# Solving the second group of four attention chunks in two half-size blocks, and filling in the corners by matmul

## The chip, the cores and the metric

One core of a Trainium2 chip runs the whole program. The metric is device time in microseconds (us). TensorE (PE) does the matmuls, VectorE (DVE), ScalarE (ACT) and GpSimd (POOL) the elementwise work, and SyncE (SP) issues most of the DMA transfers.

## The reference, cut to what matters

```
for t in range(768):                       # attention: B=4, H=8, D=40
    y[t]  = r[t] @ state
    Sa    = state @ a[t]
    state = state * w[t] - outer(Sa, b[t]) + outer(v[t], k[t])
x = y, as 3072 tokens of 320               # 8 heads x 40
x = ((x @ w1) * (x @ w2) @ w3) @ w_out     # 320 -> 1024 -> 1024 -> 320
h = max(x @ w_in, 0)                       # 320 -> 2048
out = (h * h) @ w_out2                     # 2048 -> 320
```

## The kernel before, in words

The attention runs in 24 chunks of 32 time steps. Inside a chunk the steps depend on each other through a triangular 32 by 32 system for each of the 32 pairs of batch and head. `solve(k, blocks)` inverts it ahead of time for four chunks at once, k=0 for chunks 0 to 3 and k=1 for chunks 4 to 7, and so on: four transposes in, a chain of steps on DVE (each a multiply, L666, and a subtract, L669), four transposes out. With blocks=1 the chain has 31 steps on the full triangle. With blocks=2 it has 15 steps, which treat the two 16 by 16 diagonal blocks side by side; two more transposes (`tnat`, L678) keep a copy in the other orientation, and `corner(c, i)` then fills the off-diagonal block of chunk c with two rounds of 64 small matmuls: L700 (i=0), whose result ACT scales into `x1` (L707), and L703 (i=1), whose result ACT copies into the solved tile (L711). Before the change k=0 uses two blocks, and the later solves one.

A chunk passes the stages x0, sa, sat, l, z, ys: `do_x0` (L752, ACT evicts X at L754), `do_sa` (L762, ACT copies SA at L764), `do_sat` (L769; ACT copies YI, L774, and vs, L771), `do_l` (L786, DVE writes YI, L791), `do_z` (L799, ACT copies YR, L802), `do_ys` (L814). At the end of ys DVE writes the new state, RX (L822), from which the next chunk's x0 starts, and the output yst (L826). So the chunks form one serial chain through PE, ACT and DVE. Chunks are prepared some way ahead: `prep` (scans on DVE, L564 and L574, products on POOL, L586 and L592), `prep_pq` (pq: PE L605, ACT L609, DVE L612) and `prep_kb` (kb: PE L624, ACT L628).

Between the stages the kernel works on the first feed-forward network. Early on that is `fold`, the product of w3 and w_out (PE L466, ACT L468, DVE L469), and the splitting of w1 and w2 into high and low parts: `fetch` (a DMA, L322, into `raw` or `early`; ACT L329 and L330; DVE L332 and L334), then ACT L344 for the high part and POOL L345 for the low one (`split_w`), and L357 and L358 for the last 64 rows (`split_r`). From chunk 3 on it is the matmuls `ab` (L374) and `px` (L432). After about 710 us the second network follows, on PE alone (`ph`, L374, and `po`, L1014).

The order of instructions on PE is that of the code; the table `BETWEEN` says which side works (prep, pq, kb, solve, corner) stand after which stage of chunks 0 to 3, and `pull` takes so many ns of feed-forward work. The orders on ACT, DVE, POOL and SP come from a scheduler with priorities, so a change in the table moves instructions there too, and each of these engines works its list in order.

Of the kernel before, what the change touches and what calls it, by code (L numbers as in the profile page):

```python
# [7 lines left out]
F32 = mybir.dt.float32  # L8
# [7 lines left out]
B, H, S, D = 4, 8, 768, 40  # L16
# [17 lines left out]
    (0, "start"): (("prep", 5), ("prep", 6)),  # L34
    (0, "x0"): (("corner", 0),),
    (0, "sat"): (("w3",), ("corner", 1, 0)),
    (0, "l"): (("pq", 5), ("corner", 1, 1)),
    (0, "ys"): (("kb", 5), ("pq", 6), ("kb", 6)),
    (1, "start"): (("prep", 7),),
    (1, "sat"): (("corner", 2, 0),),  # L40
    (1, "l"): (("corner", 2, 1),),
    (1, "ys"): (("pq", 7), ("kb", 7), ("solve", 1)),
    (2, "start"): (("prep", 8),),
    (2, "sat"): (("corner", 3, 0),),
    (2, "l"): (("corner", 3, 1),),
    (2, "z"): (("pq", 8), ("pull", 1300), ("kb", 8), ("pull", 1000)),
    (3, "start"): (("prep", 9),),
    (3, "z"): (("pq", 9), ("pull", 1300), ("kb", 9), ("pull", 1000)),
}
FOLD_NS = 535  # L50
SPLIT_AT = (8, 13)
# [193 lines left out]
def body(tc, img, rv, rd, vn, vp, raw, w1, w2, w3t, wo, win, wo2, ident, maskt, out, dbg=None):  # L245
# [4 lines left out]
    with (  # L250
# [12 lines left out]
        with right, tc.manual_schedule(engines={mybir.EngineType.PE}):  # L263
# [185 lines left out]
            def fold(solved):  # L449

                wf = tc.alloc_tile_pool(name="wf", bufs=1, side="right")
                wo_sb = wf.tile([128, 8, DM], F32, name="wo_sb", bufs=1)
                w3 = {}

                def load_w3(i):
                    f, g = i // 2, i % 2
                    w3[i] = fetch(wf, 4, 128, [(slice(0, 128), slice(0, 4), wcols(w3t, 128 * f, 128)[
                        512 * g:512 * g + 512, :].rearrange("(k p) f -> p k f", p=128))])

                def step(f, k):  # L460
                    if k == 0:
                        t = ps_ab.tile([128, 2, 256], F32, name="pw", tag="ab")
                        w3["ps"] = t.rearrange("p a t -> p (a t)")[:, 0:DM]
                    ps = w3["ps"]
                    i = 2 * f + k // 4
                    mm(out=ps, lhsT=w3[i][:, k % 4], rhs=wo_sb[:, k], start=(k == 0), stop=(k == 7))  # L466
                    if k == 7:
                        act.copy(out=wf_["h"][:, f], in_=ps)  # L468
                        dve.tensor_tensor(out=wf_["l"][:, f], in0=ps, in1=wf_["h"][:, f], op=ALU.subtract)  # L469

                def split12(j):
                    if not w12:
                        w12.extend([tuple(wa.tile([128, 2, FA], F32R, name=f"w{i}{n}") for n in "hl") + (
                            wa.tile([128, FA], F32R, name=f"w{i}r"),) for i in "12"])
                    for k in range(2):
                        for src, t in zip((w1, w2), w12):
                            split_w(wf, src, *t[0:2], j, k)
                    split_r(wf, [(src, 512 * j, t[2]) for src, t in zip((w1, w2), w12)])

                hold.append(solved)  # L480
                for i in range(8):
                    fetch(wf, 1, DM, [(slice(0, 128), 0, wcols(wo)[128 * i:128 * i + 128, :])], dst=wo_sb[:, i:i + 1])
                for i in range(3):
                    load_w3(i)
                hold.clear()
                items = []
                for f in range(8):
                    for k in range(8):
                        items.append((FOLD_NS, lambda f=f, k=k: step(f, k), "w"))
                        i = 2 * f + k // 4  # L490
                        if k % 4 == 3:
                            if i + W3_FIRST < 16:
                                items.append((0, lambda i=i + W3_FIRST: load_w3(i), "decode"))
                            for j in range(2):
                                if SPLIT_AT[j] == i:
                                    items.append((0, lambda j=j: split12(j), "decode"))
                return items + [(0, wf.release, "decode")], lambda: [load_w3(i) for i in range(3, W3_FIRST)]

            with (
# [134 lines left out]
                def solve(k, blocks):  # L634
# [39 lines left out]

                    def tnat(j):
                        if j == 0:
                            TT["nat"] = nat
                        dve.transpose(out=TT["nat"].rearrange("p u s -> p s u")[:, 8 * j:8 * j + 8],  # L678
                                      in_=square(T).rearrange("p t s -> p s t")[:, 8 * j:8 * j + 8])

                    items.append(init)
# [6 lines left out]

                def corner(c, i):

                    tn = TT["nat"][:, 8 * (c % 4):8 * (c % 4) + 8]
                    if i == 0:
                        TT["x1"] = ma.tile([128, H, 16], F32, name="x1", tag="x2")
                    x1 = TT["x1"]
                    ps = psat()
                    for h in range(H):
                        for b in range(B):
                            r = slice(32 * b, 32 * b + 32)
                            if i == 0:
                                mm(out=ps[r, 0, 16 * h:16 * h + 16], lhsT=Pn0[r, c % 4, h], rhs=TT[c][r, h, 16:32],  # L700
                                   start=True, stop=True, tile_position=(32 * b, 32 * b))
                            else:
                                mm(out=ps[32 * b:32 * b + 16, 0, 16 * h:16 * h + 16], lhsT=tn[r, h], rhs=x1[r, h],  # L703
                                   start=True, stop=True, tile_position=(32 * b, 32 * b))
                    v = ps[:, 0, 0:128].rearrange("p (h t) -> p h t", t=16)
                    if i == 0:
                        act.activation(out=x1, in_=v, func=AF.Copy, scale=-1.0)  # L707
                    else:
                        for b in range(B):
                            r = slice(32 * b, 32 * b + 16)  # L710
                            act.copy(out=TT[c][r, :, 16:32], in_=v[r])  # L711
# [149 lines left out]
                def run(what):  # L861
                    for op, *a in what:
                        if op == "prep":
                            prep(a[0], dve if a[0] in PD else pool)
                        elif op == "pq":
                            stage(prep_pq, a[0], a[0] % 4)
                        elif op == "kb":
                            stage(prep_kb, *a)
                        elif op == "corner":
                            for b in range(2):  # L870
                                if len(a) == 1 or a[1] == b:
                                    stage(corner, a[0], b)
# [281 lines left out]
```

## Time and profile before

| | |
|---|---|
| runs | 1073.35, 1070.08, 1073.58 us, median 1073.35 |
| profiled execution | 1070.06 us |
| its span, first to last instruction | 1068.2 us |
| around the span | 1.9 us |
| mean granted TensorE clock | 0.963 |
| PE, DVE, ACT, POOL busy | 917.6, 710.4, 441.9, 230.9 us |

The busy times are sums over the whole span, whose stages have different limits. The times in the rows count from the span's start, so an instruction at 118.97 us began 118.97 us after the first instruction.

### The profile page before, as it was taken

How to read it: one execution, taken by the hardware profiler on the slowest of the kernel's cores; microseconds unless marked ns; L12 is line 12 of the kernel's file. 1: busy time of each engine (PE TensorE's matmuls, PEld its weight loads, DVE VectorE, ACT ScalarE, POOL GpSimd, SP SyncE). 2: the span in 40 equal slices, each digit the busy share in tenths (PEclk: the TensorE clock that was granted, in tenths of full speed). 3: DMA queues.
4: the chain of work that ended last, by engine and by line, in shares of the span. 5: the costliest groups of instructions: out<-in, count | busy, mean ns of one | idle time of the engine just before them, and what ended most of it. 6: DMA issues, size and time to landing. Idle time of an engine off the chain costs nothing.

```text
span 1068.2 us, 29228 instructions
## 1 busy us (share of the span) xinstructions
PE 917.6 (86%) x12240; PEld 821.4 (77%) x12240; DVE 710.4 (67%) x1399; ACT 441.9 (41%) x943; POOL 230.9 (22%) x303
## 2 busy tenths in 40 slices
PE   1347686799989889879899999889999999999996
PEld 1235454688879779768898889878988988988886
DVE  8854889868966996896489345896455554444432
ACT  2533455343443334433343334785433333333332
POOL 0361124533334443323200000652000000000000
PEclk9999888899999999999899999989999999999999
DMA  8877775676667667656645443665123121000001
GB/s 240 297 227 200 215 225 148 157 190 163 149 151 185 161 153 192 166 155 153 161 119 111 127 97 67 174 193 99 30 62 68 46 46 25 2 25 1 24 3 27
DMA packets 209389, 134.44 MB, mean 126 GB/s; under 512 B 143793, under 2 KB 184114, under 8 KB 209252
## 3 DMA queue, kind: packets, MB, share of 16 engines
q1 hardware_dynamic: 201892, 110.61, 40.6%
q0 software_dynamic: 7072, 21.57, 7.1%
q8 instruction: 98, 1.61, 0.7%
q10 hardware_dynamic: 288, 0.33, 0.1%
q14 instruction: 39, 0.32, 0.1%
HBM read 99.27 MB, written 33.19 MB: 124 GB/s over the span
## 4 chain that ended last, share of the span: by engine, by line
PE 49%; DVE 24%; DMA 8%; issue 4%; ACT 4%; SPq 2%; POOL 2%; ACTq 0%; DVEq 0%; POOLq 0%
PE ph L374 16%; PE po L1014 15%; PE ab L374 6%; DVE T L669 4%; DVE tmp L666 3%; PE px L432 3%; DVE RX L822 2%; PE pat L814 2%; DVE yst L826 2%; DVE wst L332 2%; DMA X_d<-yst 2%; DVE wst L334 2%; DVE g L406 1%; DMA im<-img 1%; PE pat L786 1%
## 5 line engine op out<-in xcount | busy, mean ns | idle before, releaser
L1014 PE MATMUL po<-wul,rh 128*128 128x320 f32 x384 | 118.3, 308 | 0.0
L1014 PE MATMUL po<-wuh,rh 128*128 128x320 f32 x384 | 118.0, 308 | 0.0
L1014 PE MATMUL po<-wuh,rl 128*128 128x320 f32 x384 | 116.9, 308 | 0.7 <-DVE rl L1001 0.7
L411 ACT CAST gh<-g 128x256 fp32r<-128x256 f32 x96 | 38.8, 405 | 104.9 <-DVE g L406 92.5
L374 PE MATMUL ph<-xh,wih 128*128 128x512 f32 x192 | 76.0, 396 | 0.7 <-POOL wul L960 0.7
L374 PE MATMUL ph<-xh,wil 128*128 128x512 f32 x192 | 75.7, 394 | 0.0
L814 PE MATMUL pat<-YI,YR 128*40 128x72 f32 (+1 forms) x1536 | 59.0, 240 | 19.3 <-DVE qt L612 17.5
L374 PE MATMUL ph<-xl,wih 128*128 128x512 f32 x192 | 75.6, 394 | 0.0
L1014 PEld LDWEIGHTS po<-wul,rh 128*128 128x128 f32 x384 | 72.0, 188 | 4.2
L1014 PEld LDWEIGHTS po<-wuh,rh 128*128 128x128 f32 x384 | 72.0, 188 | 3.8
L814 PEld LDWEIGHTS pat<-YI,YR 128*40 128x40 f32 x1536 | 54.4, 127 | 24.9 <-DVE qt L612 19.5
L1014 PEld LDWEIGHTS po<-wuh,rl 128*128 128x128 f32 x384 | 71.6, 188 | 1.0 <-DVE rl L1001 0.9
L432 PE MATMUL px<-wph,gh 128*128 128x320 f32 x192 | 65.9, 343 | 6.9 <-ACT gh L411 3.8
L405 ACT COPY a_sb<-ab 128x256 f32<-128x256 f32 x96 | 35.6, 371 | 83.9 <-PE ab L374 83.3
L592 POOL TENSOR_TENSOR im<-im,suf 104x256 f32<-104x256 f32 x80 | 68.1, 879 | 4.7 <-DMA im<-img 2.5
L669 DVE TENSOR_TENSOR T<-T,tmp 128x31 f32<-128x31 f32 (+20 forms) x170 | 65.8, 387 | 3.1
L412 DVE TENSOR_TENSOR gl<-g,gh 128x256 fp32r<-128x256 f32 x96 | 46.9, 489 | 28.6 <-ACT gh L411 28.3
L666 DVE TENSOR_TENSOR tmp<-PT,T 128x31 f32<-128x31 f32 (+20 forms) x170 | 63.3, 372 | 3.4
L432 PE MATMUL px<-wph,gl 128*128 128x320 f32 x192 | 61.2, 319 | 2.3 <-DVE gl L412 2.2
L374 PE MATMUL ab<-xh,w1h 128*128 128x256 f32 x192 | 58.1, 303 | 2.9 <-ACT xh L361 1.9
L432 PE MATMUL px<-wpl,gh 128*128 128x320 f32 x192 | 60.5, 315 | 0.0
L374 PE MATMUL ph<-xq,wir 128*128 128x512 f32 x192 | 60.1, 394 | 0.0
(539 smaller groups left out, 2439.3 us busy)
## 6 DMA issues: line engine op xcount, KB each, us to landing
raw<-w3t SPq DMA_DIRECT2D x16, 512.0 KB
YR<-KB_d SPq DMA_DIRECT2D x48, 160.0 KB
im<-img POOLq DMA_DIRECT2D x28, 240.0 KB, 4.7
wt<-AW_d SPq DMA_DIRECT2D x24, 214.5 KB
raw<-wo SPq DMA_DIRECT2D x16, 320.0 KB
RX<-vp SPq DMA_DIRECT2D x24, 208.0 KB
vs<-rv SPq DMA_DIRECT2D x24, 208.0 KB
KB_d<-kn POOLq DMA_DIRECT2D x14, 320.0 KB, 5.1
```

Of the source, the lines that this page charges most:

```text
L332: dve.scalar_tensor_tensor(out=ou, in0=ou, scalar=3, in1=lo, op0=ALU.logical_shift_left, op1=ALU.bitwise_or)
L334: dve.scalar_tensor_tensor(out=ou, in0=hi, scalar=0x80000000, in1=ou, op0=ALU.bitwise_and, op1=ALU.bitwise_or)
L374: mm(out=ps, lhsT=seq[i][0], rhs=seq[i][1], start=(i == 0), stop=(i == 7))
L405: act.copy(out=a_sb, in_=ps[:, 0])
L411: act.copy(out=t["gh"][:, ff], in_=g)
L412: dve.tensor_tensor(out=t["gl"][:, ff], in0=g, in1=t["gh"][:, ff], op=ALU.subtract)
L432: mm(out=ps, lhsT=a_, rhs=b_, start=(k == 0 and i == 0), stop=(k == 7 and i == 2))
L592: eng.tensor_tensor(out=kb[:, g, :, :, j], in0=kb[:, g, :, :, j], in1=sg, op=ALU.mult)
L666: dve.tensor_tensor(out=tv, in0=Pv[:, :, s, s + 1:n].unsqueeze(3).to_broadcast(sh), in1=Tv[:, :, s, 0:s + 1].unsqueeze(2).to_broadcast(sh) ...
L669: return dve.tensor_tensor(out=o, in0=o, in1=tv, op=ALU.subtract).ins
L814: mm(out=ps[64 * y:64 * y + D, b, 72 * z:72 * z + n], lhsT=YR[:, u], rhs=YI[:, u, 0:n], start=True, stop=True, tile_position=(0, 64 * y))
L1014: mm(out=po[j][g], lhsT=a_, rhs=b_, start=(ff == 0 and i == 0), stop=(ff == 15 and i == 2))
```

## The change

The solve of chunks 4 to 7 goes in two blocks of 16, as that of chunks 0 to 3 did. Its corners are new: that of chunk 4 after stage ys of chunk 2, those of chunks 5, 6 and 7 between the stages of chunk 3. The corners of chunks 2 and 3, which stood between the stages of chunks 1 and 2, stand with chunk 0. The pq and kb of chunk 8 move from behind stage z of chunk 2 to behind its ys. In the split of w1 and w2 both halves of w1 come ahead of those of w2; they alternated. Two tiles change their places (`nat` of the second solve takes the buffer `x2`, `x1` one of the two of `a_sb`). The later solves are issued elsewhere in the code, in one block, before and after.

```diff
-    (0, "l"): (("pq", 5), ("corner", 1, 1)),
-    (0, "ys"): (("kb", 5), ("pq", 6), ("kb", 6)),
+    (0, "l"): (("pq", 5), ("corner", 1, 1), ("corner", 2, 0)),
+    (0, "ys"): (("corner", 2, 1), ("corner", 3, 0), ("kb", 5), ("corner", 3, 1), ("pq", 6), ("kb", 6)),
     (1, "start"): (("prep", 7),),
-    (1, "sat"): (("corner", 2, 0),),
-    (1, "l"): (("corner", 2, 1),),
     (1, "ys"): (("pq", 7), ("kb", 7), ("solve", 1)),
     (2, "start"): (("prep", 8),),
-    (2, "sat"): (("corner", 3, 0),),
-    (2, "l"): (("corner", 3, 1),),
-    (2, "z"): (("pq", 8), ("pull", 1300), ("kb", 8), ("pull", 1000)),
+    (2, "z"): (("pull", 2300),),
+    (2, "ys"): (("corner", 4, 0), ("pq", 8), ("corner", 4, 1), ("kb", 8)),
     (3, "start"): (("prep", 9),),
+    (3, "x0"): (("corner", 5, 0),),
+    (3, "sa"): (("corner", 5, 1),),
+    (3, "sat"): (("corner", 6, 0),),
+    (3, "l"): (("corner", 6, 1),),
     (3, "z"): (("pq", 9), ("pull", 1300), ("kb", 9), ("pull", 1000)),
+    (3, "ys"): (("corner", 7),),
...
-                    for k in range(2):
-                        for src, t in zip((w1, w2), w12):
+                    for src, t in zip((w1, w2), w12):
+                        for k in range(2):
                             split_w(wf, src, *t[0:2], j, k)
...
-                            TT["nat"] = nat
+                            TT["nat", k] = nat if k == 0 else ma.tile([128, 32, 16], F32, name="nat", tag="x2")
...
-                        TT["x1"] = ma.tile([128, H, 16], F32, name="x1", tag="x2")
+                        TT["x1"] = ma.tile([128, H, 16], F32, name="x1", tag="a_sb", bufs=2)
...
-                            marks[a[0]] = solve_all(a[0], 1 if a[0] else 2)
+                            marks[a[0]] = solve_all(a[0], 2)
```

Lines of the changed kernel are two higher than those named above. What the change moves is shown at three places. First PE, from the second corner round of chunk 1 (`x1_803`) to the first x0 matmuls of chunk 1 (into which `RX_97` goes). Before:

```order
L605 MATMUL pat_861<-im_601 32x64 x32
L703 MATMUL pat_899<-x1_803,early_103 16x16 x32
L814 MATMUL pat_937<-YI_509,YR_96 40x72 x16
L814 MATMUL pat_958<-YI_509,YR_96 40x72 x16
L466 MATMUL pw_981<-wo_sb_521,wst_565 128x320 x2
L624 MATMUL pat_990<-idt_63,im_601 128x104 x8
L605 MATMUL pat_1003<-im_105 32x64 x32
L624 MATMUL pat_1041<-idt_63,im_105 128x104 x8
```

After:

```order
L705 MATMUL pat_899<-x1_803,early_103 16x16 x32
L702 MATMUL pat_937<-tt_342,early_103 32x16 x32
L816 MATMUL pat_972<-YI_509,YR_96 40x72 x16
L816 MATMUL pat_993<-YI_509,YR_96 40x72 x16
L468 MATMUL pw_1016<-wo_sb_521,wst_565 128x320 x2
L705 MATMUL pat_1025<-x1_936,early_103 16x16 x32
L702 MATMUL pat_1063<-tt_342,early_103 32x16 x32
L626 MATMUL pat_1097<-idt_63,im_601 128x104 x8
L705 MATMUL pat_1110<-x1_1062,early_103 16x16 x32
L607 MATMUL pat_1147<-im_105 32x64 x32
L626 MATMUL pat_1185<-idt_63,im_105 128x104 x8
L754 MATMUL pat_1215<-RX_97,XL_511 32x40 x32
```

Four corner rounds, those of chunks 2 and 3, have come between the l stage of chunk 0 and x0 of chunk 1.

Second ACT at the start of chunk 1, whose x0 result is `X0_101`, whose SA is `SA_102`; `early` tiles hold loads of w1 and w2 (1737 and 1745 of w1, 1754 of w2), `kn` belongs to kb. Before:

```order
L628 COPY kn_991<-pat_990 128x8x40 x2
L609 COPY Pn_104<-pat_1003 128x2x4x32
L628 COPY kn_1042<-pat_1041 128x8x40 x2
L754 ACTIVATE X0_101<-pat_1071 128x320
L329 ACTIVATE wst_796<-raw_797 128x512
L329 ACTIVATE wst_1746<-early_1745 128x512
L330 ACTIVATE early_1745<-early_1745 128x512
L764 COPY SA_102<-pat_1112 128x8x40
L774 COPY YI_509<-SA_102 32x8x40 x4
```

After:

```order
L331 ACTIVATE wst_1738<-early_1737 128x512
L332 ACTIVATE early_1737<-early_1737 128x512
L630 COPY kn_1186<-pat_1185 128x8x40 x2
L331 ACTIVATE wst_1746<-early_1737 128x512
L332 ACTIVATE early_1737<-early_1737 128x512
L346 CAST w1h_1731<-wst_1738 128x512
L756 ACTIVATE X0_101<-pat_1215 128x320
L346 CAST w1h_1731<-wst_1746 128x512
L331 ACTIVATE wst_1755<-early_1754 128x512
L331 ACTIVATE wst_796<-raw_797 128x512
L346 CAST w2h_1734<-wst_1755 128x512
L766 COPY SA_102<-pat_1256 128x8x40
```

Both halves of w1's load and the cast of the first now stand ahead of X0, and the cast of a half of w2 ahead of SA.

Third ACT at the start of chunk 3 (X0 is again `X0_101`). `raw_2229` holds the last rows of the second column half of w1 and w2. Before:

```order
L344 CAST w1h_1739<-wst_2095 128x512
L468 CAST wph_70<-pw_1864 128x320
L329 ACTIVATE wst_1920<-raw_1921 128x512
L330 ACTIVATE raw_2121<-raw_2121 128x512
L754 ACTIVATE X0_101<-pat_2004 128x320
```

After:

```order
L709 ACTIVATE x1_1891<-pat_1892 128x128
L346 CAST w2h_1734<-wst_2219 128x512
L611 COPY Pn_104<-pat_1926 128x2x4x32
L331 ACTIVATE wst_2228<-raw_2229 128x512
L332 ACTIVATE raw_2229<-raw_2229 128x512
L713 COPY tt_1494<-pat_1964 16x8x16 x4
L630 COPY kn_2002<-pat_2001 128x8x40 x2
L359 CAST w1r_1733<-wst_2228 64x512
L359 CAST w2r_1736<-wst_2228 64x512
L756 ACTIVATE X0_101<-pat_2031 128x320
```

The decoding of raw_2229, the two casts of its rows (w1r, w2r), the four corner copies of chunk 4 and kb 8's copies now stand ahead of X0. On SP the load of raw_2229 stands behind the two writes of chunk 2's yst.

## Rows read from the trace of the kernel before

**Rows 1.** Windows by chunk: start, end, length, busy PE PEld DVE ACT POOL, clock, DMA.

```profile
93.30:124.60 31.30, 21.64 (x477) 15.44 (x476) 19.09 (x31) 18.42 (x38) 7.46 (x8) 0.89 0.78 218
124.60:174.50 49.90, 32.76 (x512) 23.16 (x512) 43.46 (x81) 24.45 (x48) 18.06 (x17) 0.88 0.73 212
174.50:203.40 28.90, 24.56 (x380) 19.31 (x380) 28.14 (x56) 12.84 (x26) 11.22 (x11) 0.86 0.49 133
203.40:710.00 506.60, 456.57 (x7960) 422.41 (x7960) 374.47 (x834) 215.07 (x518) 154.20 (x225) 0.95 0.60 150
```

**Rows 2.** Chain of waits, chunk 1 to chunk 3: start, us, what.

```profile
128.30 7.13 DMA xf<-X_d
...
159.94 0.49 DVE wpl L469
...
204.85 0.67 DVE tt L672
```

**Rows 3.** DVE timeline, chunk 2: start, us, line, tiles, idle before.

```profile
155.16 1.50 DVE L669 TENSOR_TENSOR T<-T,tmp 128x252 f32<-128x252 f32 x1
...
169.99 0.98 DVE L822 TENSOR_TENSOR RX<-pat,gc 40x320 f32<-40x320 f32 x2
```

**Rows 4.** Windows of L666: first solve, second solve, chunk 2 after xl.

```profile
29.00:50.50 21.50, 4.20 (x15) 1.00 0.87 284
125.00:206.00 81.00, 12.94 (x31) 0.87 0.65 185
136.10:169.90 33.80, 5.34 (x11) 0.90 0.69 211
```

**Rows 5.** The same windows, of L669.

```profile
29.00:50.50 21.50, 4.60 (x15) 1.00 0.87 284
125.00:206.00 81.00, 14.28 (x31) 0.87 0.65 185
136.10:169.90 33.80, 6.92 (x11) 0.90 0.69 211
```

**Rows 6.** Windows of all engines, chunk 2 after xl.

```profile
136.10:169.90 33.80, 24.31 (x363) 17.29 (x362) 31.45 (x52) 21.68 (x43) 12.73 (x12) 0.90 0.69 211
```

**Rows 7.** PE timeline, kb 5, a corner round, ys of chunk 3.

```profile
90.72 0.88 PE L624 MATMUL pat<-idt,im 104*128 104x104 f32 x8
...
109.46 0.69 PE L703 MATMUL pat<-x,early 32*16 32x16 f32 x64 [2.90 <-ACT x L707]
...
197.12 3.41 PE L814 MATMUL pat<-YI,YR 128*40 128x72 f32 x64 [2.96 <-DVE qt L612]
```

**Rows 8.** SP timeline, the load of half of w1.

```profile
93.48 0.41 SPq L322 DMA_DIRECT2D early<-w  x1
```

**Rows 9.** ACT timeline, chunk 1 and x0 of chunk 2.

```profile
94.24 0.44 ACT L754 ACTIVATE X<-pat 128x320 f32<-128x320 f32 x1
...
99.66 0.66 ACT L329 ACTIVATE wst<-early 128x512 f32<-128x512 f32 x1 [3.52 <-DMA early<-w]
...
100.77 0.41 ACT L764 COPY SA<-pat 128x320 f32<-128x320 f32 x1
...
103.09 0.58 ACT L771 COPY vs<-pat 104x512 f32<-104x512 f32 x1
...
111.68 1.04 ACT L711 COPY tt<-pat 16x128 f32<-16x128 f32 x4
...
130.81 0.67 ACT L330 ACTIVATE raw<-raw 128x512 uint32<-128x512 uint32 x1 [4.98 <-DMA raw<-w3t]
```

**Rows 10.** DVE timeline, chunk 1.

```profile
111.17 1.39 DVE L791 TENSOR_TENSOR YI<-pat,msk 64x512 f32<-64x512 f32 x2
...
118.97 0.99 DVE L822 TENSOR_TENSOR RX<-pat,gc 40x320 f32<-40x320 f32 x2 [2.03 <-PE pat L814]
```

**Rows 11.** ACT timeline, X0 of chunk 3.

```profile
176.26 0.44 ACT L754 ACTIVATE X<-pat 128x320 f32<-128x320 f32 x1 [6.49 <-PE pat L752]
```

**Rows 12.** POOL timeline, the first halves of w2l.

```profile
153.39 2.99 POOL L345 TENSOR_TENSOR w2l<-wst,w2h 128x512 fp32r<-128x512 f32 x2 [14.66 <-PE pat L703]
```

More of the change, by code (lines that the diff above doesn't have):

```diff
@@ L676, in tnat @@
                         if j == 0:
-                            TT["nat"] = nat
-                        dve.transpose(out=TT["nat"].rearrange("p u s -> p s u")[:, 8 * j:8 * j + 8],
+                            TT["nat", k] = nat if k == 0 else ma.tile([128, 32, 16], F32, name="nat", tag="x2")
+                        dve.transpose(out=TT["nat", k].rearrange("p u s -> p s u")[:, 8 * j:8 * j + 8],
                                       in_=square(T).rearrange("p t s -> p s t")[:, 8 * j:8 * j + 8])
@@ L689, in corner @@
                 def corner(c, i):
-                    tn = TT["nat"][:, 8 * (c % 4):8 * (c % 4) + 8]
+                    tn = TT["nat", c // 4][:, 8 * (c % 4):8 * (c % 4) + 8]
                     if i == 0:
-                        TT["x1"] = ma.tile([128, H, 16], F32, name="x1", tag="x2")
+                        TT["x1"] = ma.tile([128, H, 16], F32, name="x1", tag="a_sb", bufs=2)
                     x1 = TT["x1"]
@@ L699, in corner @@
                             if i == 0:
-                                mm(out=ps[r, 0, 16 * h:16 * h + 16], lhsT=Pn0[r, c % 4, h], rhs=TT[c][r, h, 16:32],
+                                mm(out=ps[r, 0, 16 * h:16 * h + 16], lhsT=(Pn if c > 3 else Pn0)[r, c % 4, h], rhs=TT[c][r, h, 16:32],
                                    start=True, stop=True, tile_position=(32 * b, 32 * b))
```

## The prediction, made before the changed kernel ran

> **What bounds the kernel now.** I read the windows by chunk first, then the chain of waits, then the timelines of the engines that it names. From 203 us on the kernel is PE's: 456.57 of 506.60 us busy [rows 1], and the work of that part is not changed, so what counts is when chunk 4 gets there. Ahead of it PE is busy for two thirds of the time (21.64 of 31.30 us in chunk 1, 32.76 of 49.90 in chunk 2), while DVE is busy for 43.46 of the 49.90 us of chunk 2 and for 28.14 of the 28.90 us of chunk 3 [rows 1]. The chain of waits says the same: after the load of xf ahead of chunk 2's feed-forward work, at 128.30 us, it passes through PE, and from 159.94 us to the last transpose out of the second solve at 204.85 us every named piece is DVE's [rows 2]. So DVE bounds chunks 2 and 3, and handovers through ACT and DMA bound chunk 1. I follow five points: X0 of chunk 1 at 94.24 us [rows 9], the first RX of chunk 1 at 118.97 us [rows 10], that of chunk 2 at 169.99 us [rows 3], X0 of chunk 3 at 176.26 us [rows 11], and the end of chunk 3's ys at 197.12 + 3.41 = 200.53 us [rows 7].
>
> **What DVE saves.** The second solve takes 12.94 + 14.28 = 27.22 us in its 62 steps, the first, in two blocks, 4.20 + 4.60 = 8.80 us in 30 [rows 4, 5]. That is 18.4 us less. Two further transposes of about 0.6 us each (an estimate, from the 0.67 us of a transpose out [rows 2]) leave 17.2. The question is how much of it the chain of chunks can use.
>
> **Chunk 0.** Four corner rounds now stand between l of chunk 0 and x0 of chunk 1. A round takes 0.69 us on PE [rows 7], so four take 2.8. They alternate with ACT's evictions, and I add one wait of about 0.9 us where the second round of chunk 3 comes close behind its eviction; the one such wait shown is 2.90 us [rows 7], but kb 5 stands between here. Term: +3.7, bounds +2.8 and +5.7. In chunks 1 and 2 the rounds that go away lay in PE's idle time, so I credit nothing there, and 2.8 as the bound.
>
> **Chunk 1.** X0 stood on ACT behind kb's copies. Now it stands behind the decoding of both halves of w1 and one cast. Their load waits on SP for the tile that kb 5's transposes and the corners read, and those end 3.7 later than 90.72 + 0.88 [rows 7], at 95.3. The load of a half was issued at 93.48 us [rows 8] and used at 99.66 [rows 9]: 6.2 us. So the halves land at about 101.5 to 102, and four ACT instructions of 0.66, two copies and a cast later X0 starts at about 105 in place of 94.24, +10.8. SA follows behind two casts and a decode at 107.4 to 110, in place of 100.77 [rows 9], and vs, behind buffers that POOL must free, at 112 to 116 in place of 103.09 [rows 9]. From there part is absorbed: before, l's result lay ready at about 105.3 and DVE wrote it to YI only at 111.17 [rows 10], so 5.9 us of the delay fit into a wait that was there. YR then stands behind further loads of w1 and w2. The first RX comes between 122.2 and 127.8, against 118.97 [rows 10]; I take the middle, 125.0, that is +6.0, because the load waits of this chunk (3.52 us for one [rows 9]) are neither the shortest nor the longest that it can meet. Beyond chunk 0's 3.7 this adds **+2.3**, bounds -0.5 and +5.1.
>
> **Chunk 2.** From the first RX of chunk 1 the chain goes through yst, X_d and xf (128.30 + 7.13 = 135.43 [rows 2]) to xl on DVE at about 136.1. This is not changed. From 136.1 to 169.9, 33.8 us, DVE is busy for 31.45 [rows 6]; 22 steps of the solve are 5.34 + 6.92 = 12.26 of it [rows 4, 5]. Afterwards 21 of the 30 shorter steps stand there, at 8.80 / 30 = 0.29 us each, 6.15. Now the whole solve stands ahead of RX, with four transposes more (+2.5), two decode instructions and one qt fewer (-1.8). Sum: 31.45 - 12.26 + 6.15 + 0.7 = 26.0 us busy. The 2.35 us that DVE waited I leave, which gives 28.3 in place of 33.8: **-5.5**, bound -7.8 if those waits go too. Some steps here are stretched: one of 252 columns took 1.50 us [rows 3] while POOL was in w2l from 153.39 for 2.99 us [rows 12], and 22 steps took 0.56 us on average, against 0.44 over all 62 (27.22 / 62) [rows 4, 5]. If the short steps meet the same POOL work the stretch of 22 x 0.12 = 2.6 us stays, -2.9: the upper bound.
>
> The Trainium skill, page "SBUF — State Buffer", section "SBUF: two separate sides", says that a DVE instruction with two SBUF inputs and a GpSimd instruction that reads SBUF hold one port pair exclusively, each for its whole length. The 1.50 us step beside w2l agrees. By that rule the wait doesn't shrink with the step, and the sum below would be 2.6 us higher.
>
> **X0 of chunk 3.** Before it came 176.26 - 169.99 = 6.3 us after the first RX of chunk 2 [rows 3, 11]. Now it stands on ACT behind the last rows of w1 and w2, whose load on SP follows the two writes of yst. RX and yst of both halves take about 3.7 us (the same four groups follow each other from 118.97 [rows 10] to 122.7). Three issues of 0.41 [rows 8] are 1.2. The load is half as large as the one that took 6.2, I take 5.0 (3.1 if it went by bytes). ACT then decodes it in two instructions, 1.3, copies tt for chunk 4, 1.04 [rows 9], and kn and two casts, four instructions of 0.4 to 0.66, 2.0. Sum 14.2, so **+7.9**, bounds +6.0 and +9.1.
>
> **Chunk 3.** Before, from X0 to the end of ys it took 200.53 - 176.26 = 24.3 us, DVE being full. Afterwards DVE has no solve here, and PE's work of this stretch is what bounds it: about 17.2 us with corners 5 and 6 (4 rounds, 2.8) and without those fold matmuls that now run ahead of X0, plus some 3 us of handovers. 20.3 in place of 24.3: **-4.0**, bounds -6 and 0. Corner 7 then stands ahead of x0 of chunk 4; its first round is partly hidden behind RX: +0.4. Corner 7 also ends the list: with PE busy for nine tenths from there on, the shift stays as it is.
>
> **The sum.** 3.7 + 2.3 - 5.5 + 7.9 - 4.0 + 0.4 = +4.8 us. On the profiled execution's own 1070.06 us this gives 1074.9. The median of the runs, 1073.35, lies 3.3 above that execution, so I predict 1078.2. A difference under 0.3%, 3.2 us, is about what a measurement of this kernel can't tell from none.
>
> The term of chunk 3's X0 and that of chunk 1 rest on ACT working its list in order. A row shows it: ACT waited 4.98 us for a load of w3t at 130.81 [rows 9], with X0 of chunk 2 in the list behind it. The Trainium skill, page "TensorE: Matmul & The Clock Gate", table of specifications, calls the queues of ScalarE, VectorE and GpSimdE strict FIFO, which agrees. If work could pass a waiting load, those two terms would vanish and the sum would be -5.4.
>
> **Rivals.** *Faster: the relief of DVE comes through.* If w1 lands in time, so that X0 of chunk 1 is no later than chunk 0's 3.7 (97.9 us), and if the last rows of w1 and w2 land within 6.3 us of RX, the chunks get the 17.2 us, less 3.7 for chunk 0, less 3.2 for corners 5 to 7: -10.3, 1063. For it speaks that DVE is the only engine in the chain for 45 us [rows 2]. Against it, both loads stand behind work that ends too late. Chance 0.28.
>
> *No change.* Chunk 1 absorbs all but the lower bound (-0.5) and chunk 2 gains its full 7.8: 3.7 - 0.5 - 7.8 + 7.9 - 4.0 + 0.4 = -0.3, 1073. For it speaks the 5.9 us wait of YI, which may cover more than I allow. Chance 0.18.
>
> *Slower by more.* The loads in chunk 1 queue behind each other and POOL's stretch stays: +5.1 and -2.9 in place of +2.3 and -5.5, +10.2, 1083.5. Speaks for it the DMA share of 0.78 in chunk 1 [rows 1], which is the highest of these windows. Chance 0.10.
>
> My own case has 0.44, with a range of 1074 to 1083. Of it I count 0.06 to no change, at its lower edge. So: faster 0.28, same 0.24, slower 0.48. The range that leaves out 2 in 10 runs from 1062 to 1085.
>
> **What would show it.** The two-block solve: 15 instructions each of multiply and subtract, 8 to 10 us in all. Chunk 1: X0 near 105, SA after 107, RX near 125. Chunk 2: RX 45.5 us after chunk 1's. X0 of chunk 3 about 14 us after that, with a wait for the DMA of raw ahead of it on ACT; ys ends 20 us later. The wait of w2l on corner 3 (14.66 us [rows 12]) is gone. I am wrong if X0 of chunk 1 comes before 100, or if that of chunk 3 follows RX within 8 us.

## The result, and the profile after

The changed kernel takes 1085.84 us (median of 4 runs, 1080.06 to 1089.30), the kernel before 1073.46 (4 runs): ratio 1.0124, 95% interval 1.0085 to 1.0163. It is slower, as forecast, but by 12.4 us where 4.8 were forecast. That is 2.8 us above the range of the prediction's own case (1074 to 1083) and 0.8 us above the wider one (1062 to 1085). The profiled execution took 1083.38 us, 13.3 more than that of before.

The windows by chunk, from x0 of a chunk to x0 of the next (chunks 1, 2, 3, then to the end of the attention); the columns are those of [rows 1]:

```profile
99.60:133.90 34.30, 24.54 (x353) 16.54 (x352) 29.89 (x39) 23.95 (x45) 16.56 (x14) 0.76 0.70 199
133.90:182.80 48.90, 30.72 (x512) 22.10 (x514) 36.66 (x84) 20.74 (x42) 9.30 (x11) 0.81 0.68 190
182.80:212.50 29.70, 27.11 (x764) 21.64 (x764) 11.43 (x22) 12.58 (x33) 9.83 (x13) 0.92 0.52 145
212.50:724.00 511.50, 461.57 (x7963) 427.61 (x7960) 371.69 (x828) 215.84 (x520) 152.93 (x223) 0.94 0.59 147
```

Chunk 1 has become longer, 34.3 us against 31.3 [rows 1]. In chunk 2 DVE is busy for 36.66 us in place of 43.46, yet the chunk still takes 48.9. In chunk 3 DVE's 28.14 us have fallen to 11.43, and the chunk takes 29.7 us in place of 28.9: DVE's work no longer sets the length of that chunk. The new solve itself is as short as forecast, 4.11 + 4.20 = 8.31 us for its 30 steps (windows of its lines, first L668, then L671):

```profile
130.00:170.00 40.00, 4.11 (x15) 0.87 0.68 193
130.00:170.00 40.00, 4.20 (x15) 0.87 0.68 193
```

The five points that the prediction follows, read from the timelines of ACT, DVE and PE of the changed kernel (lines are two higher than before):

```profile
99.95 0.68 ACT L331 ACTIVATE wst<-early 128x512 f32<-128x512 f32 x1 [1.47 <-DMA early<-w]
...
103.33 0.46 ACT L756 ACTIVATE X<-pat 128x320 f32<-128x320 f32 x1
...
110.45 0.62 ACT L346 CAST w2h<-wst 128x512 fp32r<-128x512 f32 x1 [3.32 <-DVE wst L336]
...
117.47 0.59 ACT L773 COPY vs<-pat 104x512 f32<-104x512 f32 x1
...
180.56 0.66 ACT L331 ACTIVATE wst<-raw 128x512 f32<-128x512 f32 x1 [3.87 <-DMA raw<-w]
...
181.66 1.05 ACT L713 COPY tt<-pat 16x128 f32<-16x128 f32 x4
...
184.66 0.44 ACT L756 ACTIVATE X<-pat 128x320 f32<-128x320 f32 x1
...
216.78 0.44 ACT L756 ACTIVATE X<-pat 128x320 f32<-128x320 f32 x1 [3.10 <-PE pat L754]
```

DVE, the first RX of chunks 1 and 2:

```profile
128.23 0.99 DVE L824 TENSOR_TENSOR RX<-pat,gc 40x320 f32<-40x320 f32 x2
...
168.08 0.98 DVE L824 TENSOR_TENSOR RX<-pat,gc 40x320 f32<-40x320 f32 x2
```

PE, x0 of chunks 1, 3 and 4, ys of chunk 3, and corner 7 between:

```profile
99.55 1.30 PE L754 MATMUL pat<-RX,XL 128*32 128x40 f32 x64
...
182.76 1.49 PE L754 MATMUL pat<-RX,XL 128*32 128x40 f32 x64 [3.89 <-ACT tt L713]
...
205.53 2.20 PE L816 MATMUL pat<-YI,YR 128*40 128x72 f32 x64
...
209.76 0.73 PE L702 MATMUL pat<-tt,Pn 32*32 32x16 f32 x64
...
211.85 0.69 PE L705 MATMUL pat<-x,nat 32*16 32x16 f32 x64 [1.37 <-ACT x L709]
...
215.56 1.16 PE L754 MATMUL pat<-RX,XL 128*32 128x40 f32 x55 [2.70 <-issue]
```

| point or stretch | before | predicted | after | step predicted | step measured |
|---|---|---|---|---|---|
| first RX of chunk 1 | 118.97 | 125.0 | 128.23 | +6.0 | +9.3 |
| from there to RX of chunk 2 | 51.0 | 45.5 | 39.9 | -5.5 | -11.2 |
| from there to X of chunk 3 | 6.3 | 14.2 | 16.6 | +7.9 | +10.3 |
| from there to the end of ys | 24.3 | 20.3 | 23.1 | -4.0 | -1.2 |
| from there to X of chunk 4 | 5.8 | 6.2 | 9.0 | +0.4 | +3.3 |
| sum, X of chunk 4 | | | | +4.8 | +10.5 |

The figures of before come from [rows 3, 7, 10, 11] and, for X of chunk 4, from ACT's timeline of before:

```profile
206.31 0.43 ACT L754 ACTIVATE X<-pat 128x320 f32<-128x320 f32 x1
```

The last 2.8 of the 13.3 us arise far behind the change. The delay shrinks to 8.8 us by chunk 19 and grows to 14.0 at chunk 23, in two stretches with nearly the same number of matmuls. The windows of these, first of before and then of after:

```profile
590.00:605.00 15.00, 12.62 (x161) 11.75 (x160) 5.45 (x11) 4.03 (x9) 0.00 (x0) 0.89 0.34 87
625.00:645.00 20.00, 17.71 (x263) 16.02 (x261) 6.98 (x15) 7.30 (x16) 0.00 (x0) 0.91 0.52 125
```

```profile
599.00:617.00 18.00, 14.85 (x158) 13.85 (x157) 5.27 (x11) 3.83 (x8) 0.00 (x0) 0.72 0.27 73
637.00:659.00 22.00, 19.19 (x265) 17.48 (x265) 7.16 (x15) 7.30 (x16) 0.00 (x0) 0.84 0.48 114
```

The granted clock, a mean over its two levels of 1.2 and 2.4 GHz, was 0.72 and 0.84 in place of 0.89 and 0.91; ahead of it TensorE had waited 3.15 us for vs and 2.65 us for xh, against 2.38 and 1.95 us before. Whether this belongs to the change can't be told from these runs: in the experiments below the time against before falls by up to 2.1 us or grows by up to 3.4 over the same chunks, and the four runs of the changed kernel lie 9 us apart.

### The profile page after: what moved, and what is told of

Its sections match the earlier page's. It is cut to its first block, busy times and chain, and to the rows that moved or that the text cites. A ratio compares the mean times of both kernels' runs of the same rounds, so it can differ in the third digit from the quotient of the medians.

```text
span 1081.5 us, 30252 instructions
## 1 busy us (share of the span) xinstructions
PE 930.4 (86%) x12752; PEld 832.9 (77%) x12752; DVE 695.2 (64%) x1369; ACT 447.6 (41%) x963; POOL 230.8 (21%) x303
## 3 DMA queue, kind: packets, MB, share of 16 engines
q1 hardware_dynamic: 201892, 110.61, 39.9%
## 4 chain that ended last, share of the span: by engine, by line
PE 47%; DVE 24%; DMA 14%; ACT 5%; issue 4%; POOL 3%; SPq 2%; ACTq 0%; DVEq 0%; POOLq 0%
PE ph L376 17%; PE po L1016 16%; PE ab L376 5%; DMA im<-img 4%; DVE tmp L668 3%; DVE T L671 3%; PE px L434 2%; PE pat L816 2%; POOL im L594 2%; DVE RX L824 2%; DVE suf L566 2%; DMA X_d<-yst 2%; DVE yst L828 2%; DMA raw<-w3t 2%; DMA early<-w 2%
## 5 line engine op out<-in xcount | busy, mean ns | idle before, releaser
L816 PEld LDWEIGHTS pat<-YI,YR 128*40 128x40 f32 x1536 | 55.0, 128 | 16.6 <-DVE qt L614 10.4
L408 DVE TENSOR_TENSOR g<-a_sb,ab 128x256 f32<-128x256 f32 x96 | 39.9, 416 | 34.6 <-ACT a_sb L407 33.8
L376 PE MATMUL ab<-xl,w1h 128*128 128x256 f32 x192 | 58.2, 303 | 1.7 <-DVE xl L364 1.7
```

The source lines that it names most:

```text
L376: mm(out=ps, lhsT=seq[i][0], rhs=seq[i][1], start=(i == 0), stop=(i == 7))
L408: dve.tensor_tensor(out=g, in0=a_sb, in1=ps[:, 1], op=ALU.mult)
L816: mm(out=ps[64 * y:64 * y + D, b, 72 * z:72 * z + n], lhsT=YR[:, u], rhs=YI[:, u, 0:n], start=True, stop=True, tile_position=(0, 64 * y))
```

## The experiments

Every ratio is to the kernel before, run on the same chip, with its 95% interval. "Theory 1" and so on are those of the expectations.

**One part at a time.** s_only has the new solve with corners 4 to 7 (and pq and kb of chunk 8 behind ys of chunk 2, as in the change); c_only the move of corners 2 and 3 into chunk 0; w_only the order of w1 and w2; sc_both the first two.

```diff
# s_only, against the change (and w1, w2 alternating, as in sc_both)
-    (0, "l"): (("pq", 5), ("corner", 1, 1), ("corner", 2, 0)),
-    (0, "ys"): (("corner", 2, 1), ("corner", 3, 0), ("kb", 5), ("corner", 3, 1), ("pq", 6), ("kb", 6)),
+    (0, "l"): (("pq", 5), ("corner", 1, 1)),
+    (0, "ys"): (("kb", 5), ("pq", 6), ("kb", 6)),
+    (1, "sat"): (("corner", 2, 0),),
+    (1, "l"): (("corner", 2, 1),),
+    (2, "sat"): (("corner", 3, 0),),
+    (2, "l"): (("corner", 3, 1),),
# c_only, against before: the lines above the other way round
# w_only, against before; sc_both, against the change, the other way round
-                    for k in range(2):
-                        for src, t in zip((w1, w2), w12):
+                    for src, t in zip((w1, w2), w12):
+                        for k in range(2):
```

> Only the second solve in two blocks, with the corners of chunks 4 to 7; corners 2 and 3 stay in chunks 1 and 2, w1 and w2 alternate as before. Theory 1 (the delay of chunk 1 comes with the move of corners 2 and 3, that of chunk 3 with the new solve and its corners): X of chunk 1 at 94 to 95 us, first RX of chunk 1 at 119 +- 1, RX of chunk 2 some 9 to 11 us earlier than before (about 160), X of chunk 3 again 14 to 17 us after it, in total -3 to +4 us. Theory 2 (the order of w1 and w2 delays chunk 1, and chunk 3's delay is only the tail of it): X of chunk 3 follows RX of chunk 2 within 8 us, and the kernel is 8 to 12 us faster than before.

Measured: 1.0051 (1.0028 to 1.0075). RX of chunk 1 at 117.2, of chunk 2 at 162.9 (7.1 earlier than before), X of chunk 3 at 178.4, 15.6 us behind it.

> Only corners 2 and 3 moved into chunk 0; the second solve in one block, w1 and w2 alternate. Theory 1: X of chunk 1 at 102 to 105 us behind two loads of w1 and w2, first RX of chunk 1 at 126 to 129, total +6 to +12 us. Theory 2: x0 of chunk 1 is later by the four corner rounds alone (+3 to +6 us), X follows it within 2 us, total 0 to +4 us.

Measured: 0.9986 (0.9959 to 1.0012). X of chunk 1 at 105.4 and RX of chunk 1 at 131.3, 12.3 late; but RX of chunk 2 is only 4.4 late, X of chunk 4 2.1. Theory 1 was right on the place and wrong on the total.

> Only w1's halves ahead of w2's. Theory 1: the order of the two loads ahead of chunk 1 changes only which weight they belong to; X of chunk 1 at 94 to 95 us, total within 3 us of before. Theory 2: X of chunk 1 at 100 us or later, total +5 to +10 us.

Measured: 0.9991 (0.9963 to 1.0020), X of chunk 1 at 93.3. Theory 2 falls.

> The whole change but the order of w1 and w2. Theory 1: like the whole change, X of chunk 1 at 102 to 105 us, total +9 to +16 us against before. Theory 2: most of the delay of chunk 1 is gone, X of chunk 1 before 99 us, total no slower than before.

Measured: 1.0150 (1.0105 to 1.0196), X of chunk 1 at 102.5. So the order of w1 and w2 does nothing that these runs can tell; it is the move of corners 2 and 3 that brings the loads of w1 and w2 ahead of X in chunk 1. And the medians of the parts don't add up: 0.51% and -0.14% alone, 1.50% together. The windows from RX of chunk 1 to RX of chunk 2, of before and of c_only, show where much of the delay of chunk 1 comes back:

```profile
119.00:170.00 51.00, 36.92 (x616) 26.23 (x612) 44.50 (x85) 28.24 (x56) 15.58 (x15) 0.90 0.73 214
```

```profile
131.30:174.40 43.10, 30.34 (x476) 21.76 (x470) 37.00 (x81) 21.27 (x42) 9.52 (x10) 0.88 0.69 202
```

DVE had 37.00 us to do there in place of 44.50. In c_only it had run 20 instructions of decoding during chunk 1, in place of 12, and had 18 left for this stretch, in place of 21. The whole change has the same 20 and 18, and there too the delay of chunk 1 comes back: RX of chunk 2 is 1.9 us earlier than before. Up to X of chunk 5 the parts do add up in the profiled executions: s_only is 6.6 us late there, c_only 1.1 and sc_both 7.8. At X of chunk 23 they are 3.9 late, 2.0 early and 7.0 late. So what sc_both has beyond the sum isn't there at chunk 5. It arises behind, where the three have the same work, and isn't explained.

**Where the new rounds stand.** TensorE's timeline of s_only, around x0 of chunk 3 (L758, behind kb 8, L630) and x0 of chunk 4:

```profile
174.62 1.65 PE L630 MATMUL pat<-idt,im 104*128 104x104 f32 x8 [4.72 <-ACT tt L717]
...
176.19 1.30 PE L758 MATMUL pat<-RX,XL 128*32 128x40 f32 x64
...
206.09 0.73 PE L706 MATMUL pat<-tt,Pn 32*32 32x16 f32 x64
...
208.19 0.69 PE L709 MATMUL pat<-x,nat 32*16 32x16 f32 x64 [1.37 <-ACT x L713]
...
211.75 1.16 PE L758 MATMUL pat<-RX,XL 128*32 128x40 f32 x55 [2.56 <-issue]
```

kb 8 waits 4.72 us for ACT to copy corner 4's second round, and x0 stands behind it. In chunk 4 corner 7's two rounds stand ahead of x0. Four kernels move them:

```diff
# s_c7, against s_only
-    (3, "ys"): (("corner", 7),),
+    (4, "sat"): (("corner", 7, 0),),
+    (4, "l"): (("corner", 7, 1),),
# s_mid, against s_only ((2, "ys") is empty; these lines take the place of those of chunk 3)
+    (3, "x0"): (("corner", 4, 0), ("pq", 8)),
+    (3, "sa"): (("corner", 4, 1), ("corner", 5, 0), ("kb", 8)),
+    (3, "sat"): (("corner", 5, 1), ("corner", 6, 0)),
+    (3, "l"): (("corner", 6, 1),),
# s_spread, against s_only, and after_spread, against the change ((2, "ys") and (3, "ys") are empty; likewise)
+    (3, "x0"): (("corner", 4, 0), ("pq", 8)),
+    (3, "sa"): (("corner", 4, 1), ("kb", 8)),
+    (3, "sat"): (("corner", 5, 0),),
+    (3, "l"): (("corner", 5, 1),),
+    (4, "x0"): (("corner", 6, 0),),
+    (4, "sa"): (("corner", 6, 1),),
+    (4, "sat"): (("corner", 7, 0),),
+    (4, "l"): (("corner", 7, 1),),
```

In the last three, prep 9 stands ahead of chunk 8's pq and kb, which thus work on chunk 9's values; the instructions are the same.

> s_only with corner 7's two rounds moved from behind ys of chunk 3 into chunk 4 (behind sat and behind l). Theory 3 (what stands on TensorE between ys and the next x0 adds in full to the chain of chunks, because corner rounds wait there for ScalarE's evictions): X of chunk 4 follows the first RX of chunk 3 by 5 to 6.5 us in place of 9.7, total 3 to 4 us under s_only, ratio to before 1.000 to 1.003. Theory 4 (the time is bound elsewhere and only the place of the wait changes): the gap shrinks, but X of chunk 5 and the total stay within 1.5 us of s_only.

Measured: 1.0026 (1.0003 to 1.0049); X of chunk 4 follows RX by 4.6 us in place of 9.7, and 2.3 us are left at chunk 5. That is theory 3 up to there. In the total it isn't shown: the ratio lies 0.25% under that of s_only, within the intervals of both, and by X of chunk 23 the two traces are level (4.2 and 3.9 us behind before).

> s_only with the group behind ys of chunk 2 (corner 4, pq 8, kb 8) moved into the stages x0 and sa of chunk 3, and corners 5 and 6 each a stage later; corner 7 stays behind ys of chunk 3. Theory 3: X of chunk 3 follows the first RX of chunk 2 by 6 to 8 us in place of 15.6, part of the 8 us comes back in chunk 3, where two or three more rounds and pq 8 and kb 8 now stand (25 to 29 us from X to the first RX in place of 24.9); total 4 to 7 us under s_only, ratio 0.997 to 1.002. Theory 4: chunk 3 takes longer by what X gains, total as s_only, ratio 1.003 to 1.008.

Measured: 1.0101 (1.0067 to 1.0136); the profiled run of it was the fastest of five, so its trace says little of the median. X of chunk 3 follows RX by 5.4 us, but 31.1 us pass from X to RX. The ratio lies above the ranges of both theories.

> The new solve with nothing between ys and x0: corner 4, pq 8, kb 8 behind x0 and sa of chunk 3, corner 5 behind its sat and l, corners 6 and 7 in chunk 4; corners 2 and 3 in chunks 1 and 2. Theory 3: X of chunk 3 at 169 to 171 us, first RX of chunk 3 at 193 to 197, X of chunk 4 at 199 to 203 (206.3 before), total 4 to 8 us under before, ratio 0.992 to 0.997. Theory 4: ratio 1.002 to 1.008 as s_only.

Measured: 1.0048 (1.0023 to 1.0073). X of chunk 3 at 170.3, 6.0 earlier than before; by X of chunk 4 only 1.6 of that are left, and the total is that of theory 4. ACT's list shows one reason, a load of w1 and w2 between X and the eviction of corner 4's first round, on which sa waits:

```profile
170.28 0.41 ACT L762 ACTIVATE X<-pat 128x320 f32<-128x320 f32 x1
...
175.26 0.65 ACT L338 ACTIVATE raw<-raw 128x512 uint32<-128x512 uint32 x1 [4.57 <-DMA raw<-w]
```

> The whole change, but with corners 4 to 7, pq 8 and kb 8 placed as in s_spread. Theory 3: chunk 1 as in the whole change (first RX at 128 +- 1), first RX of chunk 2 at 167 to 169, X of chunk 3 within 8 us of it, X of chunk 4 at 203 to 207, total within 4 us of before, ratio 0.996 to 1.003; against s_spread it shows what the move of corners 2 and 3 costs once DVE is relieved. Theory 4: as the whole change, ratio 1.010 to 1.016.

Measured: 1.0136 (1.0097 to 1.0174), no better than the change. X of chunk 3 followed RX by 5.4 us, but RX of chunk 2 came only at 173.3, and 38.8 us passed from X of chunk 3 to X of chunk 4 (32.1 in the change). Theory 3, that place alone decides, falls.

**The loads on ACT's list.** The next theory was the one that the prediction rests on: ACT stands still for loads of w1 and w2 with X behind them.

```diff
# gate1, against the change
-                    if c == 0:
+                    if c < 2:
                         gate.extend((o.ins, vs_done.ins))
# st10, against the change (gate1_st10: both; gate1_st10_c7: both, and corner 7 as in s_c7)
-SPLIT_STAGED = 8
+SPLIT_STAGED = 10
```

> The whole change, but ScalarE decodes no part of w1 or w2 before it has copied vs of chunk 1 (an order on its list; the loads are the same). Theory 5 (the loss in chunk 1 is ScalarE's list: X, SA, vs and YR of the chunk stand behind loads of w1 and w2 that have not landed): X of chunk 1 at 98 to 101 us (103.3 in the whole change), first RX of chunk 1 at 121 to 124 (128.2), of that 2 to 6 us left at X of chunk 4; ratio to before 1.006 to 1.011. Theory 6 (the weights' loading and decoding takes its time wherever it stands, so the wait only moves to chunk 2 or 3): first RX of chunk 1 earlier, first RX of chunk 2 no earlier than 168, ratio 1.010 to 1.016.

Measured: 1.0147 (1.0088 to 1.0207). X of chunk 1 at 100.5, RX of chunk 1 at 121.8, RX of chunk 2 at 164.4, as theory 5 has it; but X of chunk 3 comes at 186.3, later than in the change.

> The whole change, with all ten loads of w1 and w2 into early tiles (8 before; the last two had to wait for a free raw buffer and stood behind the writes of yst). Theory 5: ScalarE has no load ahead of X of chunk 3 to wait for; X of chunk 3 follows the first RX of chunk 2 by 9 to 13 us (16.6 in the whole change), chunk 1 as in the whole change or up to 2 us worse; ratio 1.006 to 1.012. Theory 6: X of chunk 3 still 14 to 17 us after RX, or RX of chunk 2 later by what is gained; ratio 1.010 to 1.016.

Measured: 1.0186 (1.0136 to 1.0236). X of chunk 3 follows RX by 10.8 us, as expected, but RX of chunk 2 comes at 176.1.

> Both together, in the whole change. Theory 5: the two gains add: ratio 0.999 to 1.006, X of chunk 4 at 206 to 211 us. Theory 6: ratio 1.008 to 1.016.

Measured: 1.0184 (1.0113 to 1.0255).

> Both, and corner 7 in chunk 4 as in s_c7. Theory 5: another 2 us less, ratio 0.996 to 1.004, X of chunk 4 at 201 to 207. Theory 6: ratio 1.008 to 1.016.

Measured: 1.0187 (1.0145 to 1.0229). In all four X of chunk 3 comes at 185 to 189 us, and none of the four totals is below that of the change (1.0124): theory 5 falls. In the three kernels with the edit of gate1 the solve takes the place of the load. TensorE's timelines of gate1 and gate1_st10 show it at corner 4's first round:

```profile
177.38 1.05 PE L702 MATMUL pat<-tt,Pn 32*32 32x16 f32 x64 [10.50 <-DVE tt L674]
```

```profile
179.15 1.05 PE L702 MATMUL pat<-tt,Pn 32*32 32x16 f32 x64 [13.18 <-DVE tt L674]
```

TensorE waits 10.50 and 13.18 us for the solve's last transposes, with x0 of chunk 3 behind. Before, the second solve was first needed by sa of chunk 4, and its last transpose ran at 204.85 us [rows 2]. With corner 4 ahead of x0 of chunk 3 it is due some 30 us earlier, while it is only 18 us shorter. Whether it is late then depends on what else DVE has to do in chunk 2. The windows of 130 to 170 us, first of gate1 and then of the change, show DVE full in the one and not in the other:

```profile
130.00:170.00 40.00, 28.99 (x271) 19.30 (x259) 39.21 (x72) 22.02 (x41) 15.40 (x12) 0.83 0.71 205
130.00:170.00 40.00, 29.16 (x384) 20.40 (x382) 34.24 (x81) 18.21 (x35) 8.02 (x10) 0.87 0.68 193
```

In the change itself the solve was ready in time. Its last transposes ended at 163.4 us, and corner 4's first round began behind yst (DVE, then TensorE):

```profile
162.31 1.06 DVE L674 STREAM_TRANSPOSE tt<-T 128x256 f32<-128x256 f32 x2
...
170.07 0.91 PE L702 MATMUL pat<-tt,Pn 32*32 32x16 f32 x64 [0.73 <-DVE yst L828]
```

So these kernels show what would come next once the load is gone, not what held the change. In st10, without that edit, corner 4 didn't wait for the solve either (1.42 us, behind yst); there RX itself was late.

**Without the corners.** What are those rounds worth?

```diff
# s_none, against s_only, and after_none, against the change (s_no4, against s_only: the first two lines alone)
-    (2, "ys"): (("corner", 4, 0), ("pq", 8), ("corner", 4, 1), ("kb", 8)),
+    (2, "ys"): (("pq", 8), ("kb", 8)),
-    (3, "x0"): (("corner", 5, 0),),
-    (3, "sa"): (("corner", 5, 1),),
-    (3, "sat"): (("corner", 6, 0),),
-    (3, "l"): (("corner", 6, 1),),
-    (3, "ys"): (("corner", 7),),
# s_fix, against s_spread (and SPLIT_STAGED = 10)
-    (3, "start"): (("prep", 9),),
-    (3, "sa"): (("corner", 4, 1), ("kb", 8)),
+    (3, "sa"): (("corner", 4, 1), ("kb", 8), ("prep", 9)),
```

s_no4 leaves chunk 4's off-diagonal block unsolved.

> s_only with the corner rounds of chunks 4 to 7 left out (the off-diagonal blocks of these chunks stay unsolved). Theory 7 (those rounds eat the relief: DVE's saving is usable): X of chunk 3 at 170 to 175 us (178.4 in s_only, 176.3 before), X of chunk 4 at 196 to 202 (213.0, 206.3), ratio to before 0.986 to 0.995. Theory 8 (the relief is not usable, the loads of w1 and w2 and pq, kb of chunk 8 hold chunk 3): X of chunk 4 at 204 or later, ratio 0.998 to 1.005.

Measured: 0.9958 (0.9931 to 0.9986). X of chunk 3 at 176.1 and X of chunk 4 at 203.1, both later than expected, in a profiled execution that was the slowest of ten (1072.94 against a median of 1066.83). So the relief is usable, but is worth 0.4%.

> The whole change with the corner rounds of chunks 4 to 7 left out. Theory 7: 9 to 15 us under the whole change, ratio 0.998 to 1.004; chunk 1 is as late as in the whole change, RX of chunk 2 at 167 to 169. Theory 8: at most 4 us under the whole change, ratio 1.007 to 1.016.

Measured: 1.0010 (0.9981 to 1.0039), 1.1% under the change; X of chunk 4 at 206.1 (216.8 in the change). RX of chunk 2 came at 170.7, later than expected. X of chunk 3 came at 183.9, hardly sooner than in the change (184.7): without a corner round of chunks 4 to 7 it still stood on ACT behind the load of the last rows of w1 and w2. ACT's timeline of after_none:

```profile
182.79 0.67 ACT L326 ACTIVATE wst<-raw 128x512 f32<-128x512 f32 x1 [2.87 <-DMA raw<-w]
...
183.91 0.41 ACT L751 ACTIVATE X<-pat 128x320 f32<-128x320 f32 x1
```

What the rounds cost shows from RX of chunk 2 to X of chunk 4. The lines of DVE and ACT at these two points, of after_none, s_only and s_none in turn:

```profile
170.73 0.98 DVE L819 TENSOR_TENSOR RX<-pat,gc 40x320 f32<-40x320 f32 x2
...
206.06 0.43 ACT L751 ACTIVATE X<-pat 128x320 f32<-128x320 f32 x1
```

```profile
162.88 0.98 DVE L828 TENSOR_TENSOR RX<-pat,gc 40x320 f32<-40x320 f32 x2
...
212.96 0.44 ACT L760 ACTIVATE X<-pat 128x320 f32<-128x320 f32 x1 [2.95 <-PE pat L758]
```

```profile
167.02 0.98 DVE L823 TENSOR_TENSOR RX<-pat,gc 40x320 f32<-40x320 f32 x2
...
203.06 0.43 ACT L755 ACTIVATE X<-pat 128x320 f32<-128x320 f32 x1
```

That is 35.3 us in after_none against 48.7 in the change, and 36.0 in s_none against 50.1 in s_only. Before, it was 36.3.

> s_only with corner 4 alone left out (the one ahead of x0 of chunk 3). Theory 7: X of chunk 3 at 170 to 175, 4 to 8 us of it left at X of chunk 4, ratio 0.996 to 1.001. Theory 8: X of chunk 3 within 2 us of s_only, ratio 1.003 to 1.007.

Measured: 1.0014 (0.9985 to 1.0043); X of chunk 3 at 173.9, X of chunk 4 at 207.2, 5.8 earlier than s_only. By the medians corner 4 alone is 0.4%, the other three 0.6%; both differences are about as large as the intervals allow one to tell.

> The new solve with every corner behind x0: corner 4 with pq 8 behind x0 of chunk 3, its second round with kb 8 and then prep 9 behind sa, corner 5 behind sat and l, 6 and 7 in chunk 4; ten early tiles for w1 and w2; corners 2 and 3 and the order of w1 and w2 as before. Theory 7: the rounds still cost their handovers in chunk 3, part of the relief stays: ratio 0.993 to 1.001, X of chunk 4 at 200 to 206. Theory 8: ratio 1.002 to 1.008.

Measured: 1.0017 (0.9987 to 1.0048); X of chunk 4 at 202.1, 4.2 earlier than before, in its profiled execution, which was the fastest of ten (1064.79 against a median of 1071.88). It isn't told apart from before.

TensorE's timeline of s_none, with kb 8, x0 of chunk 3 and x0 of chunk 4 (lines 625 and 753), shows what is left when the rounds are gone:

```profile
171.80 1.62 PE L625 MATMUL pat<-idt,im 104*128 104x104 f32 x8 [1.40 <-DVE yst L827]
...
174.27 1.30 PE L753 MATMUL pat<-RX,XL 128*32 128x40 f32 x64 [0.84 <-ACT kn L629]
...
201.27 0.83 PE L753 MATMUL pat<-RX,XL 128*32 128x40 f32 x64
```

x0 of chunk 3 stands behind kb 8's copies for 0.84 us, and x0 of chunk 4 runs in one piece.

No version that solves every chunk beat the kernel before; c_only, w_only and s_fix are level with it and beat the change.

## Why the prediction was wrong in size

**Chunks 0 and 1** (3.7 + 2.3 predicted, +9.3 measured). The place was right: X of chunk 1 ran at 103.33 (105 predicted), behind the decoding of w1. Two sizes were off. The four corner rounds put x0 of chunk 1 6.2 us later (99.55 against 93.33), over their bound of 5.7. vs came at 117.47, above the 112 to 116 that I allowed: ahead of SA ACT had also waited 3.32 us for DVE's decoding of w2. I put the cause partly on w1's order; w_only, c_only and sc_both show that it is the move of corners 2 and 3.

**Chunk 2** (-5.5, measured -11.2, outside the bound of -7.8). Part of the decoding had moved into chunk 1 and was no longer in the stretch: I counted two instructions fewer (with a qt 1.8 us less); there were three fewer, 12.4 us in place of 17.3. The steps of the solve took 8.31 us for 30, against 8.80 in the first solve. Of the 2.6 us that I held open for waits beside POOL about 0.9 came, since POOL's work had moved too: 9.30 us in chunk 2 in place of 18.06 [rows 1]. Two steps ran beside POOL's products, at 144.35 us for 0.75 (110 columns) and at 145.13 for 0.64 (120 columns); steps of the same widths alone took 0.27 and 0.28. That agrees with the rule of the Trainium skill, page "SBUF — State Buffer", section "SBUF: two separate sides", that such a step and a GpSimd instruction hold one port pair exclusively. Its price here was a third of what I had held open.

**X of chunk 3** (+7.9, measured +10.3). The chain was as described: the load issued behind the two writes of yst, landing 4.3 us later. SP's timeline of the changed kernel:

```profile
173.84 1.62 SPq L735 DMA_DIRECT2D wt<-AW_d  x1
175.52 0.73 SPq L831 DMA_DIRECT2D X_d<-yst  x2
176.29 0.50 SPq L324 DMA_DIRECT2D raw<-w  x1
```

The load took less than my 5.0. What I left out is ahead of it: X_d waited on SP until 175.52 behind other loads, the last of them that of wt, 3.7 us after the end of RX and yst at 171.8. So 4.5 us passed until the load was issued, where I had counted 1.2 for three issues. From its landing to X another 4.1 us went into the decoding and copies on ACT's list (4.3 predicted). after_none shows the same load ahead of X without a corner round of chunks 4 to 7.

**Luck.** Up to X of chunk 3 the sum was right to 0.1 us (184.66 against 176.26 + 8.4), but only because three errors cancel: +3.3 in chunks 0 and 1, -5.7 in chunk 2, +2.4 here. The whole of what is missing at X of chunk 4 (10.5 in place of 4.8) lies behind this point.

**Chunk 3 and x0 of chunk 4** (-4.0 + 0.4, measured -1.2 + 3.3). This is the step of the prediction that failed, the price of the corner rounds of chunks 4 to 7. I priced those of corners 5 to 7 by TensorE's time, 2.8 + 0.4 us, and of corner 4 only ACT's copy, 1.04, so 4.2 us in all. From RX of chunk 2 to X of chunk 4 my terms give 7.9 - 4.0 + 0.4 = +4.3; measured are +12.4 (48.7 us against 36.3). Without the rounds, in after_none, it is -1.0. So the rest of these terms was right to about 1 us, and the rounds cost 13.4 us in place of 4.2; s_none and s_only give 14.0. In both pairs the kernel without the rounds reaches RX of chunk 2 later, by 2.7 and 4.1 us, so that at X of chunk 4 they lie 10.7 and 9.9 apart. The medians agree with that: 1.1%, 12.2 us, by the change and after_none, 0.93%, 9.9 us of 1069, by s_only and s_none.

Eight rounds take TensorE less than 6 us. The rest is mostly waits at the handovers: each corner goes TensorE, ACT, TensorE, ACT, and kb, x0 or sa stand behind it in order (1.37 us for corner 7's x in the change, 4.72 us for corner 4's copies in s_only). Of the 13.4 us 3.4 lie ahead of X of chunk 3, 4.8 from there to the end of ys and 5.2 ahead of X of chunk 4, where I had 0.4; half of these 5.2 is a stop inside x0 (2.70 us, see the end). Some 2 of the 4.8 are fold work, which in after_none TensorE did while X still waited.

**The relief of DVE.** Of the 17.2 us that I counted, s_none lets 0.42% through, 4.5 us (1.5 to 7.4 by its interval). My rival "faster" had the right mechanism but not its worth: even without the corner rounds X of chunk 3 comes 9.1 us (s_none) and 13.2 us (after_none) behind RX of chunk 2, in place of 6.3, behind kb 8 in the one (timeline above) and the load of w1 and w2 in the other.

**Right:** the direction (at a chance of 0.48), the cost of the new solve, and that ACT's list would hold X of chunks 1 and 3. Of the rivals, "slower by more" came nearest (+10.2), though by another way: chunk 1 lost more than I gave it, but chunk 2's stretch did not stay.

**Open:** why the move of corners 2 and 3 costs 0.5 to 1% with the new solve and nothing without it. In the profiled executions sc_both lies 1.2 us behind s_only at X of chunk 5, and c_only 1.1 behind before, so DVE's work in chunk 2 doesn't explain it. after_spread lies 15.3 us behind s_spread there, and that isn't explained either. The drift behind chunk 19 isn't explained. No run prices alone that pq and kb of chunk 8 moved ahead of x0 of chunk 3, or that two tiles changed their places; both are in s_none and after_none too, so they are no part of the 10 to 14 us. The places and stretches in this part are of one profiled execution of each kernel.

## What to carry to other kernels

Price small matmul rounds that pass through another engine by their round trips and by what stands behind them in order, not by their own time: here eight rounds of 0.7 us cost 10 to 14 us. When work on the bounding engine is made shorter, ask also when its result is due: the two-block solve saved 18 us of DVE and was due some 30 us earlier, which sufficed in the change and no longer did with gate1. An experiment that leaves the suspected rounds out should be the first, not the last: it priced what twelve kernels with other places and orders had not.

## What the runs showed of the hardware that was not expected

A corner round took 1.05 us after TensorE had stood still for 10.50 us (gate1, above), against 0.73 us in its usual place in the changed kernel. The granted clock was 0.50 there (177.3 to 178.5 us), the level of 1.2 GHz, and 1.00, that of 2.4 GHz, in the changed kernel (209.7 to 212.6 us).

And x0 of chunk 4 stopped after 9 of its 64 matmuls for 2.70 us in the changed kernel and 2.56 in s_only, both marked "issue", in which TensorE waited for nothing that the profile shows; in s_none, without corner 7 ahead of it, the same 64 ran in one piece in 0.83 us. All eight kernels with corner 7 ahead of this x0 have the stop, after 9 or 10 matmuls and for 1.43 to 3.31 us; none of the others has such a stop there. Its cause stays open.
